# Block attention and a top-1 mixture of experts: the second expert fixed by a rule, the last batch's table entries written before its rows

## The chip, the cores and the metric

The kernel runs on one core of one Trainium2 chip. The metric is the device time of one execution in microseconds (us): before the change three runs took 803.38, 804.34 and 807.03 us, median 804.34. The engines are named as in the profile: PE is TensorE (matrix products and transposes; PEld its weight loads), DVE is VectorE, ACT is ScalarE, POOL is GpSimd, and SP is the engine that only issues DMAs. Each engine runs its own instructions in the order in which they stand.

## The reference

`B, H, S, D` is 8, 8, 576, 64; so there are 4608 tokens of 512 numbers, 8 experts, and 1024 hidden numbers in an expert.

```
scores = q @ k^T / sqrt(D), masked where the query's block of 64 lies before the key's
attn   = softmax(scores);  x = (attn @ v) laid out as [4608 tokens, 512]
logits = x @ w_gate;  e = argmax(logits);  gate = softmax(logits)[e]
eom    = sigmoid(x @ w_output_gate)[e]
out[t] = gate * eom * ( relu(x[t] @ w1[e]) @ w2[e] )      # only token t's own expert e
```

## The kernel before

**Attention** works on 32 pairs of heads, four pairs to a batch. For pair `p`, `softmax` (L320) makes scores and exponentials, `flip` (L410) turns the probabilities of the pair before on PE, and `values` (L446) multiplies those of the pair two before by `v`; `attend` (L964) interleaves these on PE in four rounds. Every product is kept at nearly full precision by a high and a low 16-bit half of each operand. The halves of `q` and `k` must also be turned. For pairs 0 and 1 this is done by PE: `turn_first` (L163) transposes 32-bit `q` and `k` into PSUM, and ACT and DVE write the halves. For every later pair `split_qk` (L136) makes the halves on POOL and `turn_qk` (L154) turns them by a DMA transpose on SP's queue.

**After a batch** `finish_batch` (L478) runs piece by piece beside the next pairs: router logits from the unscaled output `xT`; then the choice of expert and its weight on DVE; each token's place in a table sorted by expert, through small PE products (L562 to L567); the scaled rows (`rows`, L489: PE transposes, a DVE multiply, a DMA to `x_d`); and five indirect DMAs on POOL ("scatters", L600) that write token number and weight into the table `tab_d`.

**The experts** are worked in 21 steps: 17 of 256 tokens (P) and 4 of 128 (S), in the order of `ORDER` (L56). Each step reads its table rows (`fetch_ids`), gathers tokens from `x_d` (`fetch_x`), turns them, makes the hidden layer (`stage_h`, L918), multiplies by `w2` (`stage_y`, L945), scales on ACT into a buffer `ys` (L948), and scatters rows into the output on POOL (L949). `ys` has two buffers. `route_first` (L631) picks the fullest expert after six batches; steps 0 and 1 are its, and all their tokens but the last 128 come from those six batches, so that they can run while attention still ends. `load_first` (L822) loads that expert's weights; ACT makes the high half and POOL the low half, eight instructions of 128x1024. `route_rest` (L670) plans all other steps on DVE after the last batch has been counted, and only then are the weights of step 2 fetched (`fetch_w`, L794), their expert read from `wsel`.

What sets the order: PE's instructions around the end of attention are written out by hand (`manual_schedule`). On the other engines a scheduler places them by priority. A DMA on SP's queue also waits until the DMA eight before it has landed. Memory of the pool `sb`, released after attention, is used again by the pool `fb` for the weights `w1f`, `w2f` and the second set of halves.

The lines that the prediction speaks of: L173 and L176 (PE turns of `q` and `k`), L344 (scores), L473 (copy of `xT` on DVE), L494 (PE turns for the rows), L694 (a planning step on DVE), L807 (low halves of weights), L869 (turning gathered tokens on PE), L926 (hidden layer out of PSUM on ACT).

Of the kernel before, what the change touches and what calls it, by code (L numbers as in the profile page):

```python
# [20 lines left out]
P = 128  # L21
# [5 lines left out]
def block_attention_top1_moe(  # L27
# [44 lines left out]
    ps_t = ctx.enter_context(tc.tile_pool(name="ps_t", bufs=3, space=PSUM))  # L72
    ps_a = ctx.enter_context(tc.tile_pool(name="ps_a", bufs=1, space=PSUM))
    sb = tc.alloc_tile_pool(name="sb", bufs=2)
    small = tc.alloc_tile_pool(name="small", bufs=2)
    ld = tc.alloc_tile_pool(name="ld", bufs=2)
# [115 lines left out]
    with tc.high_priority(offset=3000):  # L192
# [16 lines left out]
        vlast = [const.tile([P, H, D], F32, name=f"vlast{i}") for i in range(2)]  # L209
        for natq, natk in nats:  # L210
# [3 lines left out]
        for vl in vlast:  # L214
            nc.gpsimd.memset(vl[64:128], 0.0)
        plast = [const.tile([P, S + 64], F32, name=f"plast{i}") for i in range(3)]
        for i in range(3):
# [260 lines left out]
    def finish_batch(b, sums, sumL, xT):  # L478
# [10 lines left out]
        def rows(t):  # L489

            r = ROWS[t]
            pm = ps_t.tile([P, 512], F32, name="ps_t")
            for g in range(NP):
                nc.tensor.transpose(pm[0:r, P * g:P * g + P], xT[:, g, Q0[t]:Q0[t] + r], ident)  # L494
            xn = sb.tile([P, DM], F32, name="xn", bufs=NT)
# [9 lines left out]
        lgT = sb.tile([P, S], F32, name="lgT", bufs=1)  # L505
        for c0, c1 in ((0, 512), (512, 576)):
            pm = ps_t.tile([P, 512], F32, name="ps_t")
            for g in range(NP):
                nc.tensor.matmul(
                    pm[32 * g:32 * g + 32, 0:c1 - c0], wg_bd[:, g, :], xT[:, g, c0:c1],  # L510
                    start=True, stop=True, tile_position=(0, 32 * g),
                )
            nc.scalar.copy(lgT[:, c0:c1], pm[:, 0:c1 - c0])
            yield
        yield
        rows(LAST)
        yield
        lh = small.tile([P, NT, H, 16], F32, name="lh", bufs=1)
# [9 lines left out]
        )  # L528
        yield
        pm = ps_t.tile([P, 512], F32, name="ps_t")  # L530
# [25 lines left out]
        yield  # L556
        for t in range(LAST):
            rows(t)
            yield

# [35 lines left out]
        for t in range(NT):  # L596
# [14 lines left out]
            if b < B - 1 and t < LAST:  # L611
                yield
                if b < B - 3:
                    yield


# [11 lines left out]
    f_i = const.tile([P, 1], I32, name="f_i")  # L628
    row0 = const.tile([P, 4], I32, name="row0")

    def route_first():  # L631
# [13 lines left out]
        nc.vector.tensor_scalar(fe, fe, float(NTOK), None, ALU.mult)  # L645
        nc.vector.tensor_scalar(row0, t64[:, 0:8:2], fe, None, ALU.add)


# [21 lines left out]
    def route_rest():  # L670

        cnt = counts(B, "cnt1")
        room, used = sb.tile([P, NPT], F32, name="pT"), [0]

# [12 lines left out]
        nk = small.tile([P, 2, E], F32, name="nk", bufs=1)  # L687
        nc.vector.tensor_reduce(nk[:, 0], big[:, :, 2:NTE:4], AX.X, ALU.add)
        nc.vector.tensor_reduce(nk[:, 1], big[:, :, 0:NTE:4], AX.X, ALU.add)
        nc.vector.tensor_tensor(nk[:, 1], nk[:, 1], nk[:, 0], ALU.subtract)  # L690

        room3 = sb.tile([P, 2, NK[3]], F32, name="pt3").rearrange("p a n -> p (a n)")[:, 0:3 * E * E].rearrange("p (k a b) -> p k a b", k=3, a=E)
        c1, cm = room3[:, 0], room3[:, 1:3]
        nc.vector.tensor_tensor(c1, upto, bc(first, [P, E, E], 1), ALU.max)  # L694
        nc.vector.tensor_tensor(cm, bc(c1, [P, 2, E, E], 1), bc(nk, [P, 2, E, E], 2), ALU.mult)
# [4 lines left out]
        nc.vector.tensor_tensor(own, nk, cum, ALU.subtract)  # L700
        nc.vector.tensor_tensor(own, own, bc(first, [P, 2, E], 1), ALU.mult)
        nc.vector.tensor_tensor(cum, cum, own, ALU.add)
        beg = small.tile([P, 2, E], F32, name="beg", bufs=1)
        nc.vector.tensor_tensor(beg, cum, nk, ALU.subtract)
        tot = small.tile([P, 2], F32, name="tot", bufs=1)
# [30 lines left out]
        nc.vector.scalar_tensor_tensor(base[:, 0], beg[:, 0], -2.0 * P, e0, ALU.mult, ALU.add)  # L736
        nc.vector.scalar_tensor_tensor(base[:, 1], nk[:, 0], 2.0 * P, e0, ALU.mult, ALU.add)
        for kind, (sl, n) in enumerate(parts):
# [21 lines left out]
    def fetch_ids(st, halves=None):  # L760
# [4 lines left out]
        lo, hi = halves or (0, n)  # L765
        row = row0[0:1, 2 * c + lo:2 * c + lo + 1] if i < 2 else rti[0:1, c:c + 1]
        with tc.issue_after(read[0].ins) if read[0] else nullcontext():
# [26 lines left out]
    def fetch_w(st):  # L794
        c = st[0]
        with chain():
            ev = nc.sync.value_load(wsel[0:1, c:c + 1], min_val=0, max_val=E - 1)
            need = nc.sync.value_load(wneed[0:1, c:c + 1], min_val=0, max_val=1)
            for src, dst in ((w1, w1f), (w2, w2f)):
                for j in range(4):  # L800
                    chained[0] = nc.sync.dma_start(
                        quarter(src, dst[j]), rows_of(src, ev, j), cond=need > 0, cond_hint=False
                    )

# [17 lines left out]
    def load_first():  # L822
# [16 lines left out]
        for c in range(4):  # L839
            load(w1, c)  # L840
        for w, fn, r0, r1 in ((w1, split_w1, 5, 1), (w2, split_w2, 2, 1)):
            for r in range(r0):
                yield
            for c in range(4):
                with tc.issue_after(last_exp[0].ins):
                    fn(nc.gpsimd, 0, wc[c], c)
                if w is w1:
                    load(w2, c)
                for r in range(r1):
                    yield  # L850

# [82 lines left out]
    def stage_y(st, halves=None):  # L934
# [58 lines left out]
    for p in range(NPR):  # L993
        b, hp = divmod(p, NP)
        if hp == 0:
            sums = small.tile([P, NT, H], F32, name="sums", bufs=3), small.tile([P, NP], F32, name="sumL", bufs=3)
            nc.gpsimd.memset(sums[0][64:128, LAST, :], 1.0)
            xT = sb.tile([P, NP, S], F32, name="xT")
        if p == NPR - 2:
# [30 lines left out]
        if p == CP:  # L1030
            with tc.issue_after(last_max[0].ins):
                constants()

    def first_tiles():
        stage_x(steps[0], (0, 1))
        yield
        stage_x(steps[0], (1, 2))
        yield
        yield from h_steps(steps[0])
# [5 lines left out]

    def beside(at):

        r = 0
        while later or r <= max(at, default=0):
            if r in at:  # L1050
                next(ahead, None)
            r += 1
            yield

    attend(iter(()))
    attend(beside((0, 1)))

    weave(beside((8, 9)))
    route_rest()
    for r in ahead:  # L1060
        pass
    fetch_ids(steps[1], (1, 2))
    fetch_x(steps[1], (1, 2))
    stage_y(steps[0])
    act = stage_x(steps[1], (1, 2))
    stage_y(steps[1], (0, 1))


    small.release()
    sb.release()  # L1070
# [5 lines left out]
    for j in range(2, NXG):  # L1076
        xg.append(fb.tile([P, 2, DM], F32, name=f"xg{j}"))
        nc.gpsimd.memset(xg[j], 0.0)

    def split_after(act, fn, src, st):  # L1080

        with tc.issue_after(act.ins):
            split_all(fn, buf(st[2]), src)

# [23 lines left out]

    fetch_w(steps[2])
    fetch_ids(steps[2])  # L1110
    for i in range(2, 2 + LX):
        fetch_ids(steps[i + 1])
        fetch_x(steps[i])
    for i in range(3 + LX, 2 + LI):
        fetch_ids(steps[i])

    turn_x(steps[2], act)
    turn_x(steps[3], act)
    act = stage_h(steps[1], (1, 2))
    split_after(act, split_w1, w1f, steps[2])  # L1120
    act = stage_y(steps[1], (1, 2))
    split_after(act, split_w2, w2f, steps[2])
    run(steps, 2)
# [43 lines left out]
```

## Time and profile before

| | us |
|---|---|
| median of three runs | 804.34 |
| the profiled execution's own time | 806.55 |
| its span, first to last instruction | 805.0 |
| PE busy, share of the span | 746.7, 93% |
| DVE, ACT, POOL busy | 534.5, 478.5, 367.1 |
| mean granted TensorE clock | 0.976 |

The span has three stages: attention alone until 339 us, the end of attention beside the first expert's two steps until 438.28 us, and the other 19 steps until 794 us; the last 11 us are the last output rows on their way. A matrix product's end is modelled, so consecutive ones seem to overlap by some hundredths. Clock 1.00 is 2.4 GHz, 0.50 is 1.2 GHz.

### The profile page before, as it was taken

How to read it: one execution, taken by the hardware profiler on the slowest of the kernel's cores; microseconds unless marked ns; L12 is line 12 of the kernel's file. 1: busy time of each engine (PE TensorE's matmuls, PEld its weight loads, DVE VectorE, ACT ScalarE, POOL GpSimd, SP SyncE). 2: the span in 40 equal slices, each digit the busy share in tenths (PEclk: the TensorE clock that was granted, in tenths of full speed). 3: DMA queues.
4: the chain of work that ended last, by engine and by line, in shares of the span. 5: the costliest groups of instructions: out<-in, count | busy, mean ns of one | idle time of the engine just before them, and what ended most of it. 6: DMA issues, size and time to landing. Idle time of an engine off the chain costs nothing. (4 is left out here: it accounts for less than half of the span.)

```text
span 805.0 us, 18665 instructions
## 1 busy us (share of the span) xinstructions
PE 746.7 (93%) x7108; PEld 524.3 (65%) x7132; DVE 534.5 (66%) x925; ACT 478.5 (59%) x1057; POOL 367.1 (46%) x343
## 2 busy tenths in 40 slices
PE   6499999999999999978975999999999999999994
PEld 4377777777667677656743765666667666676661
DVE  6366878878787978798514965766668655785530
ACT  5377676767767676763214855555567555765530
POOL 5586468594849494666364422422222323200011
PEclk9799999999999999989997999999999999999998
DMA  6989968998899848273585798585789859721601
GB/s 167 209 172 192 194 134 151 198 165 190 133 191 177 196 97 183 45 246 92 171 162 122 235 307 284 112 287 158 224 238 325 242 168 282 174 59 45 231 29 42
DMA packets 245202, 141.44 MB, mean 176 GB/s; under 512 B 199408, under 2 KB 215856, under 8 KB 245104
## 3 DMA queue, kind: packets, MB, share of 16 engines
q1 hardware_dynamic: 236288, 120.61, 63.6%
q0 software_dynamic: 8272, 19.29, 8.1%
q8 instruction: 58, 0.95, 0.6%
q14 instruction: 40, 0.33, 0.2%
q10 hardware_dynamic: 544, 0.26, 0.1%
HBM read 122.23 MB, written 19.73 MB: 176 GB/s over the span
## 5 line engine op out<-in xcount | busy, mean ns | idle before, releaser
L918 PEld LDWEIGHTS <-w1b 128*128 128x128 f16 (+1 forms) x2112 | 182.3, 98 | 23.7 <-DVE w1b L807 1.5
L945 PE MATMUL ps_t<-w2b,hh 128*128 128x512 f16 (+1 forms) x584 | 178.6, 384 | 10.1 <-ACT hh L926 10.1
L918 PE MATMUL ps_s<-xt,w1b 128*128 128x256 f16 (+3 forms) x1824 | 182.1, 262 | 0.5 <-DVE w1b L807 0.4
L807 DVE TENSOR_TENSOR w2b<-w2f,w2b 128x1024 bf16<-128x1024 f32 x76 | 88.0, 1220 | 116.4 <-ACT w2b L806 116.4
L363 DVE TENSOR_REDUCE nmx<-ps_s 128x1 f32<-128x512 f32 (+4 forms) x224 | 130.3, 615 | 44.6 <-PE ps_s L352 41.3
L356 ACT ACTIVATE pt<-ps_s,nmx 128x256 f32<-128x256 f32 (+3 forms) x256 | 132.2, 530 | 29.1 <-DVE nmx L363 26.0
L949 POOL DMA_INDIRECT out_dram<-ys,ids x38 | 46.1, 1213 | 188.0 <-ACT ys L948 125.1
L945 PE MATMUL ps_t<-w2b,hl 128*128 128x512 f16 x304 | 116.5, 383 | 1.4 <-DVE hl L927 0.2
L948 ACT ACTIVATE ys<-ps_t,ids 128x512 f32<-128x512 f32 x38 | 26.1, 687 | 151.4 <-PE ps_t L945 102.3
L945 PEld LDWEIGHTS <-hh 128*128 128x128 f16 x608 | 59.8, 99 | 79.1 <-ACT hh L926 10.2
L416 PE MATMUL ps_t<-ident,pt 128*128 128x128 f32 x640 | 100.1, 286 | 4.3 <-ACT pT L436 2.3
L416 PEld LDWEIGHTS ps_t<-ident,pt 128*128 128x128 f32 x640 | 70.7, 143 | 33.9 <-ACT pt L356 8.4
L436 ACT COPY pT<-ps_t 128x512 f32<-128x512 f32 (+1 forms) x96 | 49.4, 515 | 65.6 <-PE ps_t L416 65.6
L807 DVE TENSOR_TENSOR w1b<-w1f,w1b 128x1024 bf16<-128x1024 f32 x76 | 87.9, 1220 | 0.1
L344 PE MATMUL ps_s<-qk 64*128 64x256 f16 (+1 forms) x1152 | 71.5, 256 | 14.6 <-DMA qk<-sp 10.7
L456 PE MATMUL ps_a<-pT,vv 128*64 128x256 f32 (+3 forms) x512 | 83.7, 449 | 0.0
L780 POOL DMA_INDIRECT xg<-x_d,ids x38 | 53.4, 1406 | 54.8 <-DVE xr L884 15.4
L600 POOL DMA_INDIRECT tab_d<-idg,sli x40 | 40.4, 1011 | 78.4 <-DVE sli L581 67.6
L806 ACT CAST w1b<-w1f 128x1024 f16<-128x1024 f32 x76 | 74.2, 1045 | 0.7 <-DMA w1f<-in_moe_w_dram 0.7
L806 ACT CAST w2b<-w2f 128x1024 f16<-128x1024 f32 x76 | 73.6, 1042 | 0.0
L344 PEld LDWEIGHTS <-qk 64*128 64x128 f16 x1152 | 44.6, 95 | 37.5 <-issue 22.6
L142 POOL TENSOR_SCALAR natq<-natq 128x640 f32<-128x640 f32 x30 | 54.6, 1821 | 23.1 <-DMA natq<-in_q_dram 15.0
(183 smaller groups left out, 1041.4 us busy)
## 6 DMA issues: line engine op xcount, KB each, us to landing
w1f<-in_moe_w_dram SPq DMA_DIRECT2D x76, 512.0 KB
w2f<-in_moe_w_dram SPq DMA_DIRECT2D x76, 512.0 KB
vv<-in_v_dram SPq DMA_DIRECT2D x64, 128.0 KB
x_d<-xn SPq DMA_DIRECT2D x32, 256.0 KB
natk<-in_k_dram SPq DMA_DIRECT2D x14, 512.0 KB
natq<-in_q_dram SPq DMA_DIRECT2D x28, 256.0 KB
hh<-in_moe_w_dram SPq DMA_DIRECT2D x4, 512.0 KB
hl<-in_moe_w_dram SPq DMA_DIRECT2D x4, 512.0 KB
```

Of the source, the lines that this page charges most:

```text
L142: last_pool[0] = nc.gpsimd.tensor_scalar(qv, qv, SCALE, None, ALU.mult)
L344: nc.tensor.matmul(ps[:, ab, c:c + m], qk[rows, cq, P * t:P * t + P], cols(qk[rows, ck], x, kind), start=(i == 0), stop=(i == 2 and c + m ...
L356: last_exp[0] = nc.scalar.activation(probs[t][:, ab], ps[:, ab, c0:c0 + n], AF.Exp, bias=nmx[:, t, ab:ab + 1], accum_out=sums[:, t, 2 * hp ...
L363: last_max[0] = nc.vector.tensor_reduce(o, x, AX.X, ALU.max, negate=True)
L416: nc.tensor.transpose(ps[:, P * i:P * i + P], src, ident)
L436: copies[to](o, x if n == 1 else x.rearrange("p (j c) -> p j c", c=256))
L456: nc.tensor.matmul(pa[o, P * j:S0].rearrange("p (t n) -> p t n", n=P), vv[:, j, a0 + ab], pT[:, x:x + 256 * m].rearrange("p (t n) -> p t n ...
L780: nc.gpsimd.indirect_dma_start(out=xg[i % NXG][:, h], out_offset=None, in_=x_d[0:nx, :], in_offset=IOA(ap=ids[i][:, h, 0:1].bitcast(U32), ...
L806: nc.scalar.copy(hi, src)
L807: eng.tensor_tensor(lo, src, hi, ALU.subtract)
L918: nc.tensor.matmul(ph[:, f4].rearrange("p (h n) -> p h n", n=P), wv[:, cc, f, :], xv[:, cc], start=(k == 0), stop=(k == 3 * KD - 1))
L945: nc.tensor.matmul(py, hv[:, f, h], wv[:, f, :], start=(k == 0), stop=(k == 3 * KF - 1))
```

## The change

Four edits. (1) `turn_first` is used for pairs 1 to 3 instead of pair 1 alone, so pairs 0 to 3 are turned on PE and no DMA transpose is issued before pair 4. (2) In the last batch ("rush") all five calls of `rows` come behind the scatters, and the batch's pieces stand between groups of products of the first expert's steps, in an order written by hand. (3) The expert of step 2 is expert 0, or expert 1 where expert 0 is the first one; it is known when the first one is, so its weights are fetched as soon as `sb`'s memory is free, and its table rows and tokens with those of step 1. It is planned to have at least one step; the first expert's other steps come later, in the order of the experts. (4) The first expert's `w1` low halves are made by POOL in 16 instructions of 128x256, its `w2` low halves by DVE in four of 128x1024; `ys` has four buffers. Pools are regrouped so that `sb` can be released earlier.

```diff
-        sp = split_qk(p + 2) if p + 2 < NPR else None
-        early = turn_first(1) if p == 0 else None
+        sp = split_qk(p + 2) if NP <= p + 2 < NPR else None
+        early = turn_first(p + 1) if p + 1 < NP else None
...
+        rush = b == B - 1
...
-        for t in range(LAST):
-            rows(t)
-            yield
+        if not rush:
+            for t in range(LAST):
+                rows(t)
+                yield
...
+        if rush:
+            for t in range(NT):
+                yield
+                rows(t)
...
+        nc.vector.memset(second, 0.0)
+        nc.vector.tensor_scalar(second[:, 0:1], first[:, 0:1], -1.0, 1.0, ALU.mult, ALU.add)
+        nc.vector.tensor_copy(second[:, 1:2], first[:, 0:1])
...
+        nc.vector.scalar_tensor_tensor(cnt, second, P + 1.0, cnt, ALU.mult, ALU.max)
...
+            if st[2] == 2:
+                ev, cond = nc.sync.value_load(s_i[0:1, 0:1], min_val=0, max_val=E - 1), {}
...
+            for g in range(0, KF, 2):
+                nc.gpsimd.tensor_tensor(
+                    w1b[0][:, 1, c, g:g + 2].bitcast(BF16), wc[c].rearrange("p (g m) -> p g m", g=KF)[:, g:g + 2],
+                    w1b[0][:, 0, c, g:g + 2], ALU.subtract,
+                )
...
-            ys = fs.tile([P, DM], F32, name="ys")
+            ys = fs.tile([P, DM], F32, name="ys", bufs=4)
...
+    fetch_w(steps[2])
+
+    with tc.manual_schedule(engines=ENG):
+        for n in (1, 3, 2, 0, 1, 0, 1, 0):
+            step(rush)
+            step(ahead, n)
+        for x in rush:
+            pass
...
+        fetch_ids(steps[1], (1, 2))
+        fetch_ids(steps[2])
+        fetch_x(steps[1], (1, 2))
+        fetch_x(steps[2])
+        split_all(split_w2, 0, first_w2)
+        for x in ahead:
+            pass
+        route_rest()
+        act = stage_y(steps[0], (0, 1))
+        split_after(act, split_w1, w1f, steps[2])
+        stage_y(steps[0], (1, 2))
+        turn_x(steps[2], act)
+        stage_x(steps[1], (1, 2))
```

On SP's queue near the start, the kernel before has the first two DMA transposes (`qk` from the halves `sp`) among the loads of the second batch:

```order
L119 DMA natq_100<-in_q_dram 128x8x64
L158 DMA_TRANSPOSE qk<-sp 128x20x128
L119 DMA natq_100<-in_q_dram 128x8x64
L106 DMA natq_100<-in_q_dram 64x4x64
L106 DMA natq_100<-in_q_dram 64x4x64
L107 DMA natk_101<-in_k_dram 64x8x64
L158 DMA_TRANSPOSE qk<-sp 128x20x128
```

The changed kernel has the same loads in a row, and its first transpose, that of pair 4, behind three loads of `v`:

```order
L120 DMA natq_103<-in_q_dram 128x8x64
L120 DMA natq_103<-in_q_dram 128x8x64
L107 DMA natq_103<-in_q_dram 64x4x64
L107 DMA natq_103<-in_q_dram 64x4x64
L108 DMA natk_104<-in_k_dram 64x8x64
L314 DMA vv<-in_v_dram 64x8x64
L314 DMA vv<-in_v_dram 64x8x64
L314 DMA vv<-in_v_dram 64x8x64
L159 DMA_TRANSPOSE qk<-sp 128x20x128
```

The transposes of pairs 2 and 3 are gone, and the last loads of the second batch no longer stand behind them.

On POOL at the end of attention, the kernel before has the eight low halves with the two last batches' scatters (`tab_d`), then the table rows and tokens of step 1's second half:

```order
L807 TENSOR_TENSOR w1b_5588<-hl,w1b_5588 128x1024
L807 TENSOR_TENSOR w2b_5589<-hh,w2b_5589 128x1024
L807 TENSOR_TENSOR w2b_5589<-hl,w2b_5589 128x1024
L807 TENSOR_TENSOR w2b_5589<-hh,w2b_5589 128x1024
L600 DMA tab_d<-idg,sli 37120x2 x4
L807 TENSOR_TENSOR w2b_5589<-hl,w2b_5589 128x1024
L600 DMA tab_d<-idg,sli 37120x2 x6
L769 ISA
L769 DMA ids<-tab_d 128x2
L780 DMA xg_5592<-x_d,ids 128x512
```

The changed kernel there:

```order
L873 TENSOR_TENSOR w1b_5631<-hl,w1b_5631 128x256 x4
L607 DMA tab_d<-idg,sli 37120x2 x5
L1113 MEMSET xg_6290 128x1024
L607 DMA tab_d<-idg,sli 37120x2 x5
L793 ISA
L793 DMA ids<-tab_d 128x2
L792 TENSOR_LOAD s_i
L792 ISA x2
L793 ISA
L793 DMA ids<-tab_d 128x2x2
L804 DMA xg_5635<-x_d,ids 128x512
```

The `w2` halves have left POOL, and the table rows of step 2 are read between those of step 1 and its gather.

On SP's queue at the same place, the kernel before has the last batch's rows (`x_d`) ahead of the weights of step 2:

```order
L501 DMA x_d<-xn 64x512
L501 DMA x_d<-xn 128x512 x4
L1124 TENSOR_LOAD more
L1124 ISA x2
L797 TENSOR_LOAD wsel
```

The changed kernel has the eight weight loads first (the last three shown), then the rows:

```order
L829 DMA w2f_6285<-in_moe_w_dram 128x2x512
L829 ISA
L829 DMA w2f_6286<-in_moe_w_dram 128x2x512
L829 ISA
L829 DMA w2f_6287<-in_moe_w_dram 128x2x512
L502 DMA x_d<-xn 128x512 x4
L502 DMA x_d<-xn 64x512
```

The last batch's rows now stand behind 4 MB of weights in the same queue.

## Rows read from the trace of the kernel before

**Rows 1.** Stretches (`from:to` in us): length, busy per engine, clock, DMA share, GB/s
```profile
16.88:24.35 7.47, 6.17 (x78) 5.16 (x77) 5.39 (x10) 5.89 (x21) 7.24 (x6) 1.00 1.10 208
34.66:45.95 11.29, 11.29 (x114) 8.08 (x114) 5.47 (x10) 6.62 (x22) 8.27 (x7) 0.79 0.72 146
45.95:55.15 9.20, 9.20 (x117) 6.73 (x116) 6.08 (x11) 7.11 (x25) 8.80 (x9) 1.00 0.83 177
339.00:368.10 29.10, 22.82 (x237) 16.95 (x233) 24.82 (x45) 18.63 (x45) 19.68 (x15) 0.88 0.65 214
368.10:405.43 37.33, 35.72 (x336) 25.90 (x338) 23.12 (x85) 8.05 (x14) 17.81 (x17) 1.00 0.51 145
405.43:438.28 32.85, 19.78 (x147) 11.72 (x149) 9.38 (x11) 9.17 (x13) 16.94 (x17) 0.79 0.70 119
438.28:794.00 355.72, 354.23 (x2621) 241.42 (x2639) 227.19 (x216) 212.28 (x250) 89.61 (x71) 1.00 0.66 196
```

**Rows 2.** What PE waited for: total us, times, longest us
```profile
PE ps_s L344 <- DMA qk<-sp: 10.7, 2, 10.3
PE ps_t L945 <- ACT hh L926: 10.1, 1, 10.1
...
PE ps_t L494 <- DVE xT L473: 4.2, 1, 4.2
```

**Rows 3.** Timeline (start, length, engine): pair 1 turned; transposes of pairs 2 and 4
```profile
10.06 0.66 PE L173 MATMUL ps_t<-ident,natq 128*128 128x128 f32 x4
...
11.27 1.09 PE L176 MATMUL ps_t<-ident,natk 128*64 128x128 f32 x16
...
14.06 0.44 PE L176 MATMUL ps_t<-ident,natk 128*64 128x128 f32 x4
...
28.05 4.81 SPq L158 DMA_TRANSPOSE qk<-sp  x1
...
37.39 1.81 POOL L142 TENSOR_SCALAR natq<-natq 128x640 f32<-128x640 f32 x1 [8.14 <-DMA natq<-in_q_dram]
...
43.65 3.01 SPq L158 DMA_TRANSPOSE qk<-sp  x1
```

**Rows 4.** Stretches at half clock after idle time of PE
```profile
355.02:360.20 5.18, 5.18 (x20) 3.67 (x22) 5.05 (x16) 2.01 (x4) 2.73 (x3) 0.50 0.62 213
...
408.17:411.40 3.23, 3.23 (x10) 1.73 (x11) 0.69 (x1) 0.58 (x1) 1.76 (x2) 0.50 0.12 22
...
430.98:435.29 4.31, 4.09 (x10) 1.51 (x12) 4.18 (x5) 4.20 (x5) 3.68 (x4) 0.50 0.20 70
```

**Rows 5.** Timeline, DVE beside POOL's low halves
```profile
349.45 4.98 DVE L694 TENSOR_TENSOR pt<-upto,first 128x64 f32<-128x64 f32 x1
...
350.14 2.13 POOL L807 TENSOR_TENSOR w1b<-hh,w1b 128x1024 bf16<-128x1024 f32 x1
```

**Rows 6.** Timeline, from the last scatter to the tokens of step 1's second half
```profile
388.42 0.91 POOL L600 DMA_INDIRECT tab_d<-idg,sli  x1 [0.30 <-issue]
395.17 0.59 POOL L769 DMA_DIRECT2D ids<-tab_d  x1 [5.84 <-DMA tab_d<-idg,sli]
401.95 1.06 POOL L780 DMA_INDIRECT xg<-x_d,ids  x1 [6.18 <-DMA w2f<-in_moe_w_dram]
```

**Rows 7.** DMA issues over the whole span: count, median us from issue to landing
```profile
tab_d<-idg,sli POOLq DMA_INDIRECT x40, 6.3
xg<-x_d,ids POOLq DMA_INDIRECT x38, 4.4
...
ids<-tab_d POOLq DMA_DIRECT2D x6, 1.0 KB, 5.1
```

**Rows 8.** Timeline, first and last of twelve products of one group; the third `ys`
```profile
377.12 0.27 PE L918 MATMUL ps_s<-xh,w1b 128*128 128x256 f16 x1
...
378.32 0.27 PE L918 MATMUL ps_s<-xh,w1b 128*128 128x256 f16 x1
...
429.75 0.69 ACT L948 ACTIVATE ys<-ps_t,ids 128x512 f32<-128x512 f32 x1 [11.87 <-DMA out_dram<-ys,ids]
```

More of the change, by code (lines that the diff above doesn't have):

```diff
@@ L208, in block_attention_top1_moe @@
             ))
-        vlast = [const.tile([P, H, D], F32, name=f"vlast{i}") for i in range(2)]
+        vlast = [sb.tile([P, H, D], F32, name=f"vlast{i}", bufs=1) for i in range(2)]
         for natq, natk in nats:
@@ L215, in block_attention_top1_moe @@
             nc.gpsimd.memset(vl[64:128], 0.0)
-        plast = [const.tile([P, S + 64], F32, name=f"plast{i}") for i in range(3)]
+        plast = [sb.tile([P, S + 64], F32, name=f"plast{i}", bufs=1) for i in range(3)]
         for i in range(3):
@@ L513, in finish_batch @@
             nc.scalar.copy(lgT[:, c0:c1], pm[:, 0:c1 - c0])
+            if not rush:
+                yield
+        yield
+        if not rush:
+            rows(LAST)
             yield
-        yield
-        rows(LAST)
-        yield
         lh = small.tile([P, NT, H, 16], F32, name="lh", bufs=1)
@@ L528, in finish_batch @@
         )
-        yield
+        if not rush:
+            yield
         pm = ps_t.tile([P, 512], F32, name="ps_t")
@@ L556, in finish_batch @@
         yield
-        for t in range(LAST):
-            rows(t)
-            yield
+        if not rush:
+            for t in range(LAST):
+                rows(t)
+                yield
         pr = ps_t.tile([P, 512], F32, name="ps_t")
@@ L629, in block_attention_top1_moe @@
     row0 = const.tile([P, 4], I32, name="row0")
+    second = const.tile([P, E], F32, name="second")
+    s_i = const.tile([P, 2], I32, name="s_i")
     def route_first():
@@ L684, in route_rest @@
         nc.vector.scalar_tensor_tensor(cnt, first, 7 * 64.0 + 1, cnt, ALU.mult, ALU.max)
+        nc.vector.scalar_tensor_tensor(cnt, second, P + 1.0, cnt, ALU.mult, ALU.max)
         big = scratch([E, NTE])
         nc.vector.tensor_tensor(big, bc(cnt, [P, E, NTE], 2), bc(t64, [P, E, NTE], 1), ALU.is_gt)
[L687 to L688 removed]
+        nks = small.tile([P, 3, E], F32, name="nk", bufs=1)
+        nk, pairs = nks[:, 0:2], nks[:, 2]
+        nc.vector.tensor_reduce(pairs, big[:, :, 2:NTE:4], AX.X, ALU.add)
         nc.vector.tensor_reduce(nk[:, 1], big[:, :, 0:NTE:4], AX.X, ALU.add)
[L690 to L692 removed]
+        nc.vector.tensor_tensor(nk[:, 1], nk[:, 1], pairs, ALU.subtract)
+        nc.vector.scalar_tensor_tensor(nk[:, 0], first, -2.0, pairs, ALU.mult, ALU.add)
+        room3 = scratch([3 * E, E]).rearrange("p (k a) b -> p k a b", k=3)
         c1, cm = room3[:, 0], room3[:, 1:3]
[L694 removed]
+        nc.vector.tensor_tensor(c1, upto, bc(second, [P, E, E], 1), ALU.max)
         nc.vector.tensor_tensor(cm, bc(c1, [P, 2, E, E], 1), bc(nk, [P, 2, E, E], 2), ALU.mult)
@@ L700, in route_rest @@
         nc.vector.tensor_tensor(own, nk, cum, ALU.subtract)
-        nc.vector.tensor_tensor(own, own, bc(first, [P, 2, E], 1), ALU.mult)
+        nc.vector.tensor_tensor(own, own, bc(second, [P, 2, E], 1), ALU.mult)
         nc.vector.tensor_tensor(cum, cum, own, ALU.add)
         beg = small.tile([P, 2, E], F32, name="beg", bufs=1)
+        nc.vector.tensor_scalar(cum[:, 0], cum[:, 0], 2.0, None, ALU.add)
         nc.vector.tensor_tensor(beg, cum, nk, ALU.subtract)
@@ L736, in route_rest @@
         nc.vector.scalar_tensor_tensor(base[:, 0], beg[:, 0], -2.0 * P, e0, ALU.mult, ALU.add)
-        nc.vector.scalar_tensor_tensor(base[:, 1], nk[:, 0], 2.0 * P, e0, ALU.mult, ALU.add)
+        nc.vector.scalar_tensor_tensor(base[:, 0], first, 4.0 * P, base[:, 0], ALU.mult, ALU.add)
+        nc.vector.scalar_tensor_tensor(base[:, 1], pairs, 2.0 * P, e0, ALU.mult, ALU.add)
         for kind, (sl, n) in enumerate(parts):
@@ L765, in fetch_ids @@
         lo, hi = halves or (0, n)
-        row = row0[0:1, 2 * c + lo:2 * c + lo + 1] if i < 2 else rti[0:1, c:c + 1]
+        row = row0[0:1, 2 * c + lo:2 * c + lo + 1] if i < 2 else s_i[0:1, 1:2] if i == 2 else rti[0:1, c:c + 1]
         with tc.issue_after(read[0].ins) if read[0] else nullcontext():
@@ L840, in load_first @@
             load(w1, c)
[L841 to L850, printed above, removed]
+        for r in range(5):
+            yield
+        for c in range(4):
+            with tc.issue_after(last_exp[0].ins):
+                nc.scalar.copy(w1b[0][:, 0, c], wc[c].rearrange("p (g m) -> p g m", g=KF))
+            for g in range(0, KF, 2):
[3 more added lines that the diff above has]
+                )
+            load(w2, c)
+            yield
+        first_w2.extend(wc[c] for c in range(4))
+    first_w2 = []
     def buf(i):
@@ L1032, in block_attention_top1_moe, with split_after @@
                 constants()
+    def split_after(act, fn, src, st):
+        with tc.issue_after(act.ins):
+            split_all(fn, buf(st[2]), src)
     def first_tiles():
[L1035 to L1038, printed above, removed]
         yield from h_steps(steps[0])
@@ L1044, in block_attention_top1_moe, with both_x @@
     ahead = first_tiles()
[L1046 to L1069, printed above, removed]
+    def both_x(r):
+        if r > 1:
+            stage_x(steps[0], (r - 2, r - 1))
+    attend(iter(()), both_x)
+    hp, b, pT, vab, sums, xT = prods.pop()
+    ended = values(hp, pT, *vab, xT)
+    rush = finish_batch(b, *sums, xT)
+    with tc.manual_schedule(engines=ENG):
+        for r in range(2):
+            step(ended)
+            for g in list(later):
+                for n in range(2):
+                    step(g)
+            step(ahead)
+        step(ended)
+    assert not any(True for g in later for x in g)
     sb.release()
@@ L1077, in block_attention_top1_moe @@
         xg.append(fb.tile([P, 2, DM], F32, name=f"xg{j}"))
[L1078 to L1083, printed above, removed]
+    fetch_w(steps[2])
+    with tc.manual_schedule(engines=ENG):
+        for n in (1, 3, 2, 0, 1, 0, 1, 0):
[3 more added lines that the diff above has]
+            pass
+        for j in range(2, NXG):
+            nc.gpsimd.memset(xg[j], 0.0)
+        fetch_ids(steps[1], (1, 2))
[11 more added lines that the diff above has]
+        stage_x(steps[1], (1, 2))
+        act = stage_y(steps[1], (0, 1))
+        split_after(act, split_w2, w2f, steps[2])
+        for i in range(3, 2 + LX):
+            fetch_ids(steps[i])
+            fetch_x(steps[i])
+        for i in range(2 + LX, 2 + LI):
+            fetch_ids(steps[i])
+        act = stage_h(steps[1], (1, 2))
+        turn_x(steps[3], act)
+        stage_y(steps[1], (1, 2))
     def run(seq, i0):
@@ L1107, in run @@
         stage_y(seq[n - 1])
[L1109 to L1122, printed above, removed]
     run(steps, 2)
```

24 lines of the change are left out of this document (14 added, 10 removed).

## The prediction

> **What bounds the kernel now.** I read the busy shares first: PE 93% of the span, no other engine above 66%. So time can only come from PE's idle time, from half clock, or from PE's work. The table by stages [rows 1] says where that is. In the last stage (438.28 to 794) PE is busy 354.23 of 355.72 us at full clock: nothing is to be had there, and the change leaves its products as they are. From 45.95 to 339 the pairs run one behind the other, 9.20 us each. The loss lies in three places. At the start, pair 2 begins at 34.66 where pair 1 ended its PE work at 24.35. From 339 to 368.10 PE is busy 22.82 of 29.10. From 368.10 to 438.28 it is busy 35.72 + 19.78 of 70.18. The list of PE's waits names the releasers [rows 2]: the DMA transpose of `qk` (10.3 at once), ACT's `hh` (10.1), DVE's `xT` (4.2). A gather of `xg` is the fourth, from 405.43 to 408.17 [rows 1, 4]. After each long one the granted clock is 0.50 for some us [rows 4]: the price is half of PE's busy time there, 2.6, 1.6 and 2.0; pair 2 took 11.29 where pair 3 took 9.20, 2.1 more [rows 1].
>
> **Part 1, pairs 2 and 3 turned on PE.** The wait for `qk` goes. In its place comes PE work: per pair the groups that pair 1 shows, 0.66 + 1.09 + 0.44, and one more turn of `q`, a quarter of the 0.66: 2.4 us [rows 3]. Pair 1's stretch then is 6.17 busy + 2.4 for turning pair 2 + some 0.6 of waits for ACT (half of the 1.30 idle there now, since the turning fills part of it) = 9.2, ending at 26.1. Pair 2's is 9.20 + 2.4 = 11.6, ending at 37.7, where it now ends at 45.95: 8.2 us gained. ACT and DVE get eight instructions a pair more; ACT is busy 5.89 of 7.47 and 7.11 of 9.20 now [rows 1]. If all of 1.30 stays and pair 2 waits 1 us too, the gain is 6.5; with no wait it is 8.8. What is late next is pair 4, the first that still goes over POOL and a DMA transpose. PE wants it at 37.7 + 9.2 = 46.9. Now POOL starts on it at 37.39, held by a `natq` load, and its transpose is issued at 43.65, 6.3 later; pair 2's transpose was issued at 28.05 and PE went on at 34.66, 6.6 later [rows 1, 3]. The `natq` load stood on SP's queue behind pair 2's transpose, which held that queue for 4.81 [rows 3] and is gone. With the load 4 us earlier pair 4 is there at 33.4 + 6.3 + 6.6 = 46.3, just in time: an estimate. Should it not come earlier, PE waits 3.4 us there, and the gain is 4.8.
>
> **Part 2, 339 to 368.10.** PE idles 6.28 and loses 2.6 to half clock, 8.9 in all [rows 1, 4]. The 4.2 behind `xT` is a planning step of DVE, L694, that took 4.98 while POOL ran two low halves of 2.13, and `xT` stood behind it [rows 5]; the rest, 2.1, I take to be of the same kind. In the change L694's heir stands later, behind the `w1` halves, and POOL's pieces are a quarter as long, 0.53 by size. Nine such two-input operations remain beside them; if each waits half a piece and PE feels the worse half, 2 us are left, without half clock: 6.5 gained. Bounds: none left, 8.9; blocked over whole chunks as L694 was, which started before the first of its two POOL instructions and ended only after the second, 3.
>
> The Trainium skill (SBUF — State Buffer, Who interferes with whom) says that the port pair shared by DVE and GpSimd is an exclusive lock, held for a whole instruction, that goes to whichever starts first. By that rule DVE would get in at the end of any piece and under 1 us would stay lost, making the sum 1 us better. The L694 row differs: it missed a border between two POOL instructions [rows 5]. I stay at 2.
>
> **Part 3, 368.10 to 438.28.** PE's work is the same set of products: 55.5 busy, of which 1.6 + 2.0 is half clock, so 51.9 at full clock [rows 1, 4]. Added to it are new waits. The long one, 10.1, goes: ACT stood 11.87 us in front of the third `ys`, waiting for an output scatter to land [rows 8], and `hh` stood behind it; with four buffers that wait begins at the fifth `ys`, a step later. Its half clock, 2.0, goes with it. The weights of step 2, now fetched before the plan is made, were not what PE waited for, so that edit by itself brings nothing here; it moves 4 MB out of the stretch in which table rows and tokens are fetched.
>
> What is late next is the second half of step 1, whose tokens hang on the last batch's scatters. The chain now: last scatter at 388.42, rows asked for at 395.17, tokens at 401.95, PE at 408.17 [rows 4, 6], 19.8 us, beside those 4 MB. In the change the batch's routing stands behind six groups of twelve products where it stood behind two, and its five turns of rows come later. A group is 1.3 us (1.20 from the first to the last start, eleven steps) [rows 8], a turn some 0.55 (four of the 0.66 row's kind, without the overlap [rows 3]): the last scatter comes 4 × 1.3 − 5 × 0.55 = 2.5 us later in PE's order, 20.3 + 2.5 = 22.8 after the stage's start. The weights are issued some 5 us into the stage, when the last pair's values are done; at the 196 to 214 GB/s of the table [rows 1] 4 MB take 20 us and are mostly through by then. With the medians of the whole span, 6.3 + 5.1 + 4.4 = 15.8 [rows 7], tokens are there at 38.6; with today's 19.8, at 42.6. PE reaches the place after the same work as now, 37.33 with 1.6 idle [rows 1], so at 37 to 38. I take a wait of 1, from 0 to 5.
>
> Smaller waits: DVE gets four low halves of `w2` and all five row products between the first expert's tiles; POOL made the former beside free DVE time. DVE is busy 23.12 of 37.33 [rows 1], but each piece in front of an `xl` or `oh` can cost PE up to 1.2; I count 0.3 + 0.8 + 1.3 + 0.5 = 2.9 for the four places at which PE's product follows such a piece in the written order. The sum is 51.9 + 1 + 2.9 = 55.8 against 70.18: 14.4 gained; I take 14, from 9 (wait 5, its half clock 1.6, half an us more each) to 17.
>
> **The steps.** The rule may pad expert 0 to one step of 256, and a plan of more than 17 such steps would start the extra loop. Counted from the reference's inputs, experts have 896, 0, 1030, 58, 512, 192, 384 and 1536 tokens: expert 2 is first, expert 0 second with three steps of its own, the plan has 17 + 4 steps as before. One load of weights fewer is needed. Costed at nothing: PE hides it [rows 1].
>
> **The sum.** 8.2 + 6.5 + 14 = 28.7. The profiled execution took 806.55 (its span 805.0), so 778 for such a one; the median of the runs is 2.2 lower, 804.34, which gives 776 (775.6).
>
> **Rivals.**
> - *The tokens come late.* The weights hold up rows and table entries: the last rows now stand on SP's queue behind 4 MB. Against it: 20 us at the table's rates, and rows are asked for some 23 us into the stage. For it: today's chain is slower than the medians [rows 6, 7]. PE waits 5 to 10, plus 2 of half clock: 783 to 789, say 785.
> - *DVE stays blocked.* POOL's pieces follow each other without a gap, DVE gets in only after a chunk: part 2 brings 3 and part 3 loses 2 more by late `xl`: 782. For it the L694 row, against it that its successor stands elsewhere.
> - *PE's turning lowers the clock.* Pairs 1 and 2 will have 6.17 + 2.4 + 11.6 = 20 us of PE work, more of it transposes than anywhere in the trace. Were half of it done at clock 0.50, it would take 10 us more, the start's gain would be gone, and the time 785. Against it: pair 1's stretch, with flips by transposing, has clock 1.00, and so has pair 3's [rows 1]. For it speaks the Trainium skill (TensorE: Matmul & The Clock Gate, Part 4: PE-mode transpose): transposes don't count as PE work for the clock as other products do. By the rows above the trace does not bear this out so far.
> - *Slower.* One mechanism: SP's queue. The weights wait for memory that attention frees; if one of its last readers comes late, the rows behind them on the same queue come late, and so all gathers. Its price is PE's wait at the second half of step 1; it decides only beyond 28 us there, that is when the rows land over 66 us into the stage. 4 MB would have to take 40 us more than reckoned. 808.
> - *It doesn't do what it says*: `ys` was not the cause, and the scatter's slow landing blocks ACT at the fifth buffer: part 3 loses 8 of its 14: 784.
>
> **Chances.** Forecast (771 to 780) 0.6; tokens late 0.15; DVE blocked 0.1; `ys` again 0.06; clock 0.04; slower 0.03; better than 771 0.02. The range runs from 769 (all best ends: 8.8 + 8.9 + 17 = 34.7, rounded down) to 789 (the tokens at their latest). Half a per cent, 4 us, is about what this kernel's runs can tell from no change: faster 0.95, same 0.02, slower 0.03.
>
> **What would show it.** In the changed profile: no PE wait for `qk` of 10 us and clock 1.00 from 30 to 50 us; pair 4 without a wait; no DVE two-input step over 1 us between 330 and 360; no ACT wait before the third `ys`; PE's wait for `xg` under 3 us; the last stage again some 356 us long. I am wrong if PE idles over 6 us between the first expert's tiles, if a wait for `qk` returns at pair 4, or if the last stage has grown.

## The result and the profile after

The changed kernel takes 791.12 us (median of six runs, 788.92 to 795.93); six runs of the kernel before, on the same chip, have a median of 805.39. The ratio is 0.9836, with a 95% interval from 0.9802 to 0.9869: 13 us faster by the ratio, 14 by the medians. The forecast was 28 us faster, 776 us, with a range from 769 to 789; the measured time lies just outside it. The profiled execution took 793.01 us, its span 791.1.

By stages, the changed kernel (columns as in [rows 1]; the last row covers most of the pairs in one piece):

```profile
16.88:26.06 9.18, 8.31 (x104) 6.60 (x104) 6.72 (x13) 7.69 (x26) 0.00 (x0) 1.00 1.19 210
26.06:36.85 10.79, 10.79 (x136) 7.82 (x135) 8.11 (x18) 8.61 (x29) 1.74 (x1) 1.00 0.96 184
46.79:339.68 292.89, 280.85 (x3394) 202.28 (x3393) 224.93 (x513) 201.88 (x650) 190.78 (x172) 1.00 0.91 161
339.68:367.49 27.81, 21.49 (x216) 16.16 (x218) 22.72 (x44) 16.97 (x38) 17.79 (x24) 0.94 0.65 197
367.49:425.32 57.83, 51.15 (x476) 35.24 (x479) 36.83 (x104) 19.92 (x29) 24.27 (x26) 1.00 0.62 152
425.32:781.00 355.68, 354.20 (x2621) 241.86 (x2639) 223.46 (x213) 208.76 (x247) 92.76 (x78) 1.00 0.65 187
...
56.00:330.00 274.00, 262.82 (x3174) 190.05 (x3175) 212.30 (x479) 187.78 (x604) 180.62 (x164) 1.00 0.92 163
```

The two middle stages of the kernel before, cut at the same instructions (pair 4's first score to the last pair's, then to the end of the counting products of the seventh batch):

```profile
55.15:340.60 285.45, 279.80 (x3394) 202.57 (x3393) 222.39 (x508) 201.63 (x650) 185.43 (x169) 1.00 0.84 162
340.60:368.10 27.50, 21.23 (x207) 15.59 (x206) 24.43 (x43) 17.03 (x39) 18.78 (x15) 0.88 0.68 226
```

Pair 4 begins at 46.79 instead of 55.15: the start's gain is there, 8.4. But the same 3394 products of pairs 4 to 30 then take 292.89 us instead of 285.45, so the last pair begins only 0.9 us earlier. Of these 7.4 us, 4.9 are more waits for `qk`, 1.3 more waits for copies by ACT and DVE, and 1.1 more busy time of PE. Its stretch takes 27.81 instead of 27.50 (1.3 of it is the turning of the first two tiles of tokens, which came later before). The next stage takes 57.83 instead of 70.18, the last is unchanged. What PE waited for (columns as in [rows 2]):

```profile
PE ps_t L417 <- ACT pT L437: 7.7, 7, 5.1
PE ps_s L345 <- DMA qk<-sp: 5.3, 6, 1.5
...
PE ps_s L949 <- ACT xh L901: 2.3, 2, 2.0
PE ps_s L949 <- DVE xl L902: 2.3, 3, 1.3
...
PE ps_a L900 <- DMA xg<-x_d,ids: 1.0, 1, 1.0
```

The one wait of 10 us for `qk` has become six short ones, spread over the pairs. One of 5.1 for a copy of ACT is new. Where they come from can be followed in the timeline. First pair 11's `qk`, from POOL to PE (start, length, engine, and in brackets the idle time before):

```profile
100.91 1.12 POOL L607 DMA_INDIRECT tab_d<-idg,sli  x1 [12.44 <-DVE sli L588]
102.10 1.81 POOL L143 TENSOR_SCALAR natq<-natq 128x640 f32<-128x640 f32 x1
...
109.68 5.86 SPq L159 DMA_TRANSPOSE qk<-sp  x1
...
120.69 0.34 PE L345 MATMUL ps_s<-qk 64*128 64x128 f16 x6 [1.47 <-DMA qk<-sp]
```

POOL stood 12.44 us in front of a batch's first scatter, and pair 11's split behind it; its transpose went out 11.0 us before PE began pair 11, and was 1.47 late. In the kernel before it went out only 9.5 us ahead, and PE did not wait:

```profile
116.18 4.24 SPq L158 DMA_TRANSPOSE qk<-sp  x1
...
125.66 0.34 PE L344 MATMUL ps_s<-qk 64*128 64x128 f16 x6
```

So the transpose was wanted 9.5 us after its issue in both kernels; what grew is the time that it took to land. Then the stall at 355, where DVE, POOL, ACT and PE meet:

```profile
353.18 4.47 DVE L484 COPY sums<-sumL 64x4 f32<-64x4 f32 x1
353.20 2.55 POOL L873 TENSOR_TENSOR w1b<-hh,w1b 128x256 bf16<-128x256 f32 x4
...
355.72 2.53 POOL L873 TENSOR_TENSOR w1b<-hl,w1b 128x256 bf16<-128x256 f32 x4
...
359.01 1.04 ACT L832 CAST w2b<-hh 128x1024 f16<-128x1024 f32 x1 [5.24 <-DMA hh<-in_moe_w_dram]
359.22 0.68 DVE L437 COPY pT<-ps_t 128x512 f32<-128x512 f32 x1
359.96 0.36 ACT L437 COPY pT<-ps_t 128x256 f32<-128x256 f32 x1
...
360.38 1.11 PE L417 MATMUL ps_t<-ident,pt 128*128 128x128 f32 x4 [5.08 <-ACT pT L437]
```

DVE's small copy stood 4.47 us beside POOL's pieces (0.15 is its shortest time elsewhere), and ACT stood 5.24 us for a load of `w2` in front of its own copy. Both copies of `pT` end near 360; the profile names ACT's, which came last by 0.4 us. It takes an experiment to say whether either alone would have done it.

### The profile page after: what moved, and what is told of

The parts are those of the page before. It is cut to its first block, busy times and chain, and to the rows that moved or that the text cites. A ratio compares the mean times of both kernels' runs of the same rounds, so it can differ in the third digit from the quotient of the medians.

```text
span 791.1 us, 18769 instructions
## 1 busy us (share of the span) xinstructions
PE 746.1 (94%) x7159; PEld 524.4 (66%) x7182; DVE 539.4 (68%) x946; ACT 480.6 (61%) x1065; POOL 346.3 (44%) x341
## 5 line engine op out<-in xcount | busy, mean ns | idle before, releaser
L976 PE MATMUL ps_t<-w2b,hh 128*128 128x512 bf16 (+1 forms) x585 | 175.9, 379 | 0.0
L833 DVE TENSOR_TENSOR w2b<-w2f,w2b 128x1024 bf16<-128x1024 f32 x76 | 88.0, 1220 | 113.6 <-ACT w2b L832 113.6
L980 POOL DMA_INDIRECT out_dram<-ys,ids x38 | 43.3, 1139 | 178.9 <-ACT ys L979 116.3
L417 PE MATMUL ps_t<-ident,pt 128*128 128x128 f32 x640 | 99.4, 283 | 11.1 <-ACT pT L437 7.7
L833 DVE TENSOR_TENSOR w1b<-w1f,w1b 128x1024 bf16<-128x1024 f32 x76 | 88.3, 1218 | 0.3 <-ACT w1b L832 0.3
L143 POOL TENSOR_SCALAR natq<-natq 128x640 f32<-128x640 f32 x28 | 51.0, 1822 | 34.1 <-DVE pT L437 25.6
```

The costliest lines, as they stand in the source:

```text
L143: last_pool[0] = nc.gpsimd.tensor_scalar(qv, qv, SCALE, None, ALU.mult)
L417: nc.tensor.transpose(ps[:, P * i:P * i + P], src, ident)
L833: eng.tensor_tensor(lo, src, hi, ALU.subtract)
```

## The experiments

The expectations name theories by letters: A and D say that with PE ahead the DMA side can't deliver the pairs faster, L that DVE is locked out by POOL. In the table, "lead" is how much earlier PE makes the last products with `v` (L470 in the changed kernel) for pair 1 and for pair 29 than in the profiled execution of the kernel before; "waits" is PE's total wait for `qk` from 56 to 345 us. Each ratio is to runs of the kernel before made beside that kernel, whose medians were 804.0 to 805.4.

| kernel | edit 1 | lead at pair 1, 29 | waits | median us | ratio (95%) |
|---|---|---|---|---|---|
| before | no | 0, 0 | 0.4 | 805.39 | |
| changed | yes | 8.4, 0.9 | 5.3 | 791.12 | 0.984 (0.980 to 0.987) |
| 1 before + edit 1 | yes | 8.3, 0.0 | 4.2 | 806.23 | 1.000 (0.997 to 1.003) |
| 2 changed − edit 1 | no | 1.1, 0.7 | 0.0 | 792.00 | 0.983 (0.976 to 0.989) |
| 3 scatters later | yes | 8.3, −3.9 | 5.3 | 800.31 | 0.993 (0.989 to 0.996) |
| 4 `w1` low halves on DVE | yes | 8.4, 0.7 | 7.1 | 790.52 | 0.980 (0.974 to 0.987) |
| 5 `v` loaded twice only | yes | 8.0, 6.2 | 1.1 | | |
| 6 two `ys` | yes | 8.4, 0.6 | 7.6 | 793.09 | 0.984 (0.975 to 0.993) |
| 7 before + four `ys` | no | 1.8, 1.6 | 0.2 | 794.05 | 0.984 (0.975 to 0.992) |
| 8 `w2` casts later | yes | 8.2, 2.4 | 3.6 | 789.54 | 0.980 (0.972 to 0.988) |
| 9 4 and 8 together | yes | 8.4, 0.2 | 3.9 | 785.90 | 0.976 (0.971 to 0.981) |
| 10 9 − edit 1 | no | 0.2, 0.8 | 0.2 | 788.67 | 0.983 (0.977 to 0.990) |
| 11 weights late | yes | 6.4, 1.9 | 3.3 | 805.52 | 1.000 (0.996 to 1.004) |

**1 and 2, edit 1 alone and all but edit 1.** The diff is the change's own first one, applied to the kernel before and undone in the changed one.

> The kernel before with edit 1 alone (pairs 2 and 3 turned on PE). In the changed kernel pair 4 began 8.4 us earlier than before, and the last pair only 0.9 us earlier. Theory A (supply at its limit: with PE 8 us ahead the DMA engines cannot deliver the later pairs faster, the lead is eaten again): the lead at the last pair is under 2 us, PE waits for `qk` 4 us or more in total, the time is 802 to 804. Theory B (the lost lead has nothing to do with edit 1; it was chance in that execution or came with the other edits): the lead at the last pair is still 6 to 8 us, waits for `qk` under 2 us, the time 796 to 799.

> The changed kernel without edit 1 (pairs 2 and 3 over POOL and the DMA transpose again). Theory A: edit 1 is worth about 1 us there, so the time is 791 to 793, and the pairs run as in the kernel before with under 1.5 us of waits for `qk` behind pair 3. Theory B: edit 1 is worth 6 to 8 us, so the time is 797 to 800 if the waits for `qk` came by chance; if they come with the other edits they show here too, 4 to 5 us behind pair 3, and the time is above 800.

Theory A both times. Alone, edit 1 changes nothing that can be measured (806.23 lies above the range of theory A, but the kernel before took 804.80 beside it), and without it the changed kernel is as fast within its interval. Every kernel of the table with edit 1 loses most of its lead, but the one that moves fewer bytes (5); no kernel without it waits more than 0.4 us for `qk` behind pair 3.

**3, the scatters later.**

```
+        if b < B - 3:
+            for r in range(4):
+                yield
         for t in range(NT):      # the five scatters
```

> The changed kernel with the five scatters of batches 0 to 4 four rounds later in the written order. POOL stood 12.4 us before the first scatter of a batch, and the split of pair 11's `q` and `k` stood behind it, so that its DMA transpose went out only 11 us before PE wanted it. Theory S (the supply of `qk` is late because POOL's queue holds the split behind the scatter): the transposes of pairs 11, 15, 19, 23 go out 5 us or more earlier against their use, the waits for `qk` fall from 5.3 us to about 1.5, the time is 786 to 788. Theory D (the DMA engines are the bound between 56 and 330 us; they were busy 251 us of 274, where before 235): waits move elsewhere, the time stays at 790 to 792.

Theory S fell. POOL's split of pair 11 ended at 97.48 instead of 109.65, and pair 11 waited no more. But then the transposes stood on SP's queue behind loads and rows: that of pair 19 went out 12.8 us after its split, and PE waited longer than ever:

```profile
201.62 7.18 SPq L159 DMA_TRANSPOSE qk<-sp  x1
...
210.98 0.50 PE L345 MATMUL ps_s<-qk 64*128 64x128 f16 x6 [3.50 <-DMA qk<-sp]
```

The time was 800.31, worse than either expectation; some 4 us of that arose behind the pairs and weren't followed up. Nor were all of the 12 us of lead that it lost in the pairs: the waits for `qk` are 5.3 of them.

**4, `w1` low halves on DVE.**

```
-            for g in range(0, KF, 2):
-                nc.gpsimd.tensor_tensor(w1b[0][:, 1, c, g:g + 2]..., ALU.subtract)
+            nc.vector.tensor_tensor(w1b[0][:, 1, c]..., ALU.subtract)
```

> The changed kernel with the first expert's `w1` low halves made by DVE in four instructions of 128x1024 instead of by POOL in 16 of 128x256. In the changed kernel a 64x4 copy on DVE (L484) took 4.47 us while POOL's pieces ran, and PE stood 5.08 us there. Theory L (DVE was locked out by POOL's pieces): no DVE instruction there takes over 1.5 us, PE's idle time from 339 to 367 us falls from 6.3 to about 2, half clock (1.7) goes, the time is 784 to 787. Rival (ACT was the cause: its cast of `w2` stood 5.24 us waiting for its load in front of the copy that PE waited for): the load still comes late, PE still waits 4 us or more, 789 to 792. Rival (DVE, now with 4.9 us more work, becomes late for the copies): 791 to 794.

The stall at 355 went: from the last pair's first score to the counting products it took 23.6 us (339.94 to 363.56) instead of 27.8, without half clock. In the profiled executions 2.6 of these 4.2 us reached the end (spans of 788.5 and 791.1): DVE, late in the last batch's routing, now kept PE 2.72 us in front of one product. The medians, 790.52 and 791.12, don't tell the two kernels apart. So the stall's cause was POOL's work, but the run doesn't tell DVE's lock from ACT's late load, which came earlier too.

**5, `v` for two batches only.** From batch 2 on the values of batches 0 and 1 are used again; so other tokens go to other experts, the plan gets longer, and only the part up to 340 us can be compared (the whole takes 964.14).

```
+        if b > 1:
+            values_of[b] = values_of[b % 2]
+            return
```

> The changed kernel, but `v` is loaded for batches 0 and 1 only and later batches use these again: 7 MB of the 45 MB that the pairs move between 56 and 330 us are left out, no instruction of an engine. Theory D (with PE 8 us ahead the DMA engines bound the pairs: the bytes moved by a given time are the same with the lead as without): waits for `qk` behind 56 us fall from 5.3 us to under 1.5, the lead over the kernel before at the last pair is 6.5 to 8 us instead of 0.9, the time 784 to 786. Rival C (the chain from the batch's routing over POOL's queue to the DMA transpose sets when `qk` is there, whatever the DMA engines carry): waits of 4 to 6 us stay, 790 to 792.

Theory D, though the lead is a little under its range: 1.1 us of waits is left, and the lead stays at 6.2 to the end of the pairs. No engine's instruction is missing (but SP's queue has the loads of `v` less, so the run doesn't part the bytes from the queue), and the chain over POOL's queue is as before (pair 19's transpose goes out 9.5 us before its use, and PE doesn't wait). The DMA columns fall against those of the changed kernel in the same stretch, 0.92 and 163:

```profile
56.00:330.00 274.00, 267.05 (x3221) 191.95 (x3219) 214.67 (x495) 191.28 (x617) 182.20 (x165) 1.00 0.74 139
```

**6 and 7, `ys`.** The buffers of the change back to two, and four of them alone in the kernel before.

> The changed kernel with two buffers of `ys` instead of four. If the four buffers are what removed the wait of 10.07 us (and 2.0 us of half clock behind it), PE idles 8 to 11 us again in front of a product of `w2` near 415 to 430 us, and the time is 800 to 803. Rival: in the new order the output rows of the first steps lie further apart, so two buffers do nearly as well: under 3 us, 791 to 794.

> The kernel before with four buffers of `ys` and nothing else. If the wait of 10.07 us was all that stood there, it goes with its 2.0 us of half clock: 792 to 794. Rival: what ACT does next (the first halves of step 2, the next weights) was late as well and PE waits for that, so under 5 us come of it: 799 to 803.

Alone, the four buffers bring 10 us between medians (794.05 against 804.02; by the ratio's interval 6 to 19); in the new order they bring 2 (793.09 against 791.12, within the spread). The changed order had already parted the output rows: with two buffers ACT's third `ys` stood 1.02 us, not the 11.87 of [rows 8]:

```profile
415.42 0.69 ACT L979 ACTIVATE ys<-ps_t,ids 128x512 f32<-128x512 f32 x1 [1.02 <-issue]
```

**8, the casts of `w2` later on ACT.**

```
-        split_all(split_w2, 0, first_w2)
+        with tc.issue_after(x_act[0].ins):       # the second tile's conversion
+            split_all(split_w2, 0, first_w2)
```

> The changed kernel with ACT's four casts of the first expert's `w2` placed behind the conversion of the second tile of tokens, instead of in front of the copies of the last pair. In the changed kernel the first of these casts stood 5.24 us waiting for its load, in front of a copy that PE waited 5.08 us for; DVE was locked out for 4.47 us in the same stretch, and its own copy ended 0.4 us before ACT's. Theory ACT: PE's wait there falls below 1.5 us, the 2.0 + 0.46 behind the second tile go too: 784 to 786. Theory L (DVE locked out by POOL's pieces is enough by itself): PE's wait there is still 4 to 4.8 us, only the 2.5 go: 788 to 790.

Theory L: ACT's wait is gone, DVE's lock is not, and PE still stood 5.14 us. Another instruction of DVE was caught, a 128x40 one whose shortest time is 0.19, and smaller ones behind it waited too:

```profile
351.30 2.56 POOL L873 TENSOR_TENSOR w1b<-hh,w1b 128x256 bf16<-128x256 f32 x4
...
351.99 3.80 DVE L558 TENSOR_TENSOR oh<-er,erev 128x40 f16<-128x40 f32 x1
...
353.82 2.54 POOL L873 TENSOR_TENSOR w1b<-hl,w1b 128x256 bf16<-128x256 f32 x4
...
356.69 2.58 POOL L873 TENSOR_TENSOR w1b<-hh,w1b 128x256 bf16<-128x256 f32 x4
356.79 0.62 DVE L579 TENSOR_TENSOR run_cnt<-run_cnt,add 128x8 f16<-128x8 f16 x1
...
358.15 0.52 DVE L601 SCALAR_TENSOR_TENSOR zs<-zs,se 128x5 f32<-128x5 f32 x1
358.59 0.68 DVE L498 TENSOR_TENSOR xn<-ps_t,rec 128x512 f32<-128x512 f32 x1
...
359.37 1.09 PE L900 MATMUL ps_t<-ident,xg 128*128 128x128 f32 x4 [5.14 <-POOL w1b L873]
```

The bracket in the last row names POOL, one of whose pieces ended at that moment. What that product needs is a PSUM buffer of `ps_t`, of which there are three in turn, and its buffer is the one that DVE's L498 had finished with at 359.27. L498 stood behind the operations that POOL held up. These rows also show two kinds of hold. L558 stood through six pieces that followed one another, but L579 was done at 357.41, where the first of the next four pieces ended at 357.39, and L601 at 358.67, where the third ended at 358.64: they got in at the end of one piece, though the next followed without a gap.

**9 and 10, both together, with and without edit 1.**

> Both edits of the last stretch together: the first expert's `w1` low halves on DVE, and ACT's casts of `w2` behind the second tile of tokens. With the late casts alone PE still stood 5.14 us while DVE was locked out (one 128x40 operation took 3.80 us beside POOL's pieces) and ran 3.4 us of its work at half clock. If that lock is all that is left there, PE's idle time from the last pair's start to the first expert's tiles falls below 3.5 us, half clock goes, and the time is 5 to 7 us under the 789.5 of the late casts alone: 782 to 785. Rival (DVE, with 4.9 us more to do, is late for the copies of the last pair and for the routing of the last batch): small waits of 3 to 4 us in all, 786 to 789.

> The kernel of the run before this one without edit 1 (pairs 2 and 3 over POOL and the DMA transpose). If the lead of edit 1 is always eaten by the DMA engines, it costs nothing to leave it out: within 2 us of the other. If the losses of the lead in the executions seen so far were chance, it is 4 to 7 us slower.

785.90 is the fastest measured here, 19 us under the kernel before and 5 under the changed one. It is 1 us above the first theory's range and at the lower end of the rival's: the stall and the half clock went, and small waits came. The longest left between 340 and 425 us are two of 1.3; one of them is in the third of these rows of what PE waited for:

```profile
PE ps_t L417 <- DVE pT L444: 3.8, 5, 0.8
...
PE ps_t L417 <- ACT pT L437: 1.9, 6, 0.3
PE ps_s L948 <- DVE xl L901: 1.8, 2, 1.3
```

Without edit 1 it takes 788.67. The medians differ by 2.8 us, between the two expectations, and the means by 5.0, since two of its six runs took 795.63 and 798.02; the intervals overlap. So these two runs settle neither expectation; that edit 1 is worth little rests on runs 1 and 2.

**11, the weights of step 2 late.**

```
-            if st[2] == 2:
+            if False:
...
         route_rest()
+        fetch_w(steps[2])
```

> The changed kernel, but the weights of step 2 are fetched as in the kernel before, after the plan, their expert read from the plan; the second expert stays fixed by the rule. The prediction took the early fetch by itself as worth nothing: 790 to 793. Rival: fetched late, the 4 MB run beside the table rows and tokens of step 1's second half again, PE waits 2 to 4 us more for these tokens (1.05 in the changed kernel), with half clock behind it: 794 to 797.

Neither: 805.52, the whole gain lost. The loads go out at 408.11, when the plan is done, and ACT's casts of them stand in front of the conversion of the tokens that PE wants:

```profile
411.57 1.04 ACT L832 CAST w1b<-w1f 128x1024 f16<-128x1024 f32 x1 [3.89 <-DMA w1f<-in_moe_w_dram]
414.61 1.04 ACT L832 CAST w1b<-w1f 128x1024 f16<-128x1024 f32 x1 [1.99 <-DMA w1f<-in_moe_w_dram]
...
418.92 0.58 ACT L901 CAST xh<-ps_a 128x512 f16<-128x512 f32 x1
```

PE stood 8.45 us there, worked at half clock until 424.31, and stood 2.06 more at step 2. In the kernel before the plan was done, and these loads went out, at 391 us; in the new order the plan stands behind the first expert's tiles. The early fetch is what makes that order pay as it is written; another place for these casts was not tried.

## Why the prediction was wrong, step by step

| step | forecast | measured |
|---|---|---|
| part 1, the start | 8.2 | 8.4 at pair 4, 0.9 at the last pair |
| part 2, the last pair | 6.5 | 1.0 (27.50 − 27.81 + 1.26 of turning moved into it) |
| part 3, the first expert | 14 | 11.1 (70.18 − 57.83 − 1.26) |
| sum | 28.7 | 13.0 |

**Part 1: the sum added what was gained at pair 4 to the end.** Its own working was right: 9.18 and 10.79 us for the two stretches (9.2 and 11.6 forecast), pair 4 without a wait, clock 1.00 throughout, so that the rival of a lowered clock fell. The step that failed is the sentence "the pairs run one behind the other, 9.20 us each". 9.20 is pair 3 alone: pairs 4 to 30 took 285.45 us, 10.57 each, of which PE was busy 10.36. Above all, it read PE's busy time as a bound that stands alone, and did not ask what else has a rate there. The DMA share of [rows 1], 0.83 for one pair, stood in the same row. Runs 1, 2 and 5 show that the lead is eaten, and that most of it comes back when the DMA side has less to move; without the 10.3 us wait at pair 2 the late transposes miss their turn by 0.2 to 3.5 us each. That this wait had given the transfers time is a reading, not shown. Not settled is what in the DMA side binds: the engines (share 0.91 here, but 1.19 with 210 GB/s from 16.88 to 26.06, so 163 GB/s is not the most that they can move), the order of SP's queue (which decided run 3) with its limit of eight DMAs, or both.

**Part 2: the rival of a blocked DVE came true, and went further than its price.** It was given 3 us of gain instead of 6.5; 1.0 was measured. The step that failed is the estimate that each operation waits half a piece of POOL's. One did not: the copy L484 got in only after seven pieces in a row, L558 in run 8 after six, and these holds are most of the two stalls (4.47 of 5.08 us, 3.80 of 5.14). Others did wait for one piece at most, as estimated (L579 and L601 in run 8). Why some get in at a border and some don't is open. The Trainium skill (SBUF — State Buffer, Who interferes with whom) gives the port pair to whichever instruction starts first, for that whole instruction. The trace agrees for L579 and L601. It doesn't for L484, which is recorded 0.02 us before POOL's first piece and did not get in at the end of any of the first six. ACT's cast in front of its copy, which run 8 shows was not needed for the stall, had no term at all: I had counted `w2`'s low halves on DVE, and not that their high halves on ACT wait for loads which wait for POOL's `w1`.

**Part 3: the size was near, in part by luck; the account of it was not right.** PE idled 6.7 us there, where 3.9 was forecast: the tokens came 1.05 late (1 forecast, and the whole rival of late tokens fell); the four places at which I had counted 2.9 for DVE came to some 3; 2.46 was ACT again, its last `w2` cast waiting for its load in front of the second tile. No half clock was left. But the term for `ys`, 10.1 and 2.0, was credited to the four buffers, and run 6 shows that the new order alone brings nearly all of it. And the early weights, costed at nothing, are worth 14 us in this order (run 11). They were judged in the kernel before, where the plan comes 17 us earlier than in run 11.

**Its sums, redone.** Part 3's lower end does not follow from its terms: 14.4 less 4 (a wait of 5 instead of 1), 1.6 and four times 0.5 is 6.8, not 9. The rival of late tokens, 4 to 9 us more wait and 2 of half clock, gives 782 to 787, not 783 to 789. With either put right, 791.12 still lies outside.

**What held.** The last stage, 355.68 against 355.72; 21 steps; no ACT wait of that kind before the third `ys`; the queue of SP as a source of a slowdown fell. Of the three signs of being wrong one came: PE idled 6.7 us in the stage of the first expert's tiles, over the 6 that were named.

## What to carry to other kernels

A gain early in a long pipeline is only kept if every supplier of that pipeline has room; before adding it to the sum, read the DMA share of the steady stretch, and look for the transfer that lands just when it is wanted. When DVE work that PE waits for runs beside a row of POOL instructions, don't count on the borders between them: cut to a quarter, they still held one operation for seven pieces. Moving them to another engine took the stall away here (runs 4 and 9). Edits that remove the same wait don't add up, and an edit worth nothing in the old order can be what the new order stands on: judge each in the order it will run in.

## What the runs showed of the hardware that was not expected

DVE stood through seven POOL instructions of 0.67 us that followed one another (4.47 us for a 64x4 copy) and through six (3.80 for a 128x40 operation), about as long as through two of 2.13 in the kernel before [rows 5]. Yet it got in at the end of single ones too, and then it was POOL that waited. In the changed kernel DVE's L833 took its usual 1.21 us, and POOL's piece beside it 1.72 instead of 0.67, so that three pieces took 2.98:

```profile
361.08 1.21 DVE L833 TENSOR_TENSOR w2b<-hh,w2b 128x1024 bf16<-128x1024 f32 x1
361.10 2.98 POOL L873 TENSOR_TENSOR w1b<-hl,w1b 128x256 bf16<-128x256 f32 x3
```

DVE's copy out of PSUM at 359.22, beside POOL's pieces, took the usual 0.68. From 56 to 330 us the DMA engines moved 163 GB/s in every kernel with edit 1 and 165 or 166 in those without, but for run 5, at busy shares from 0.84 to 0.92: PE's lead raised the rate nowhere. That goes with the loss of the lead, and doesn't by itself say what caused it. In the kernel before, 124,771 of the 143,494 packets there were of 256 bytes, 32 of the 45 MB.
